# Keeping the split weights of a layer's first pass in DRAM for its second pass, in a three-layer kernel on one core

## The chip, the cores and the metric

The kernel runs on one core of a Trainium2 chip. The metric is the device time of one execution in microseconds (us), less is better. Times of single stretches come from one profiled execution.

## The reference

Linear attention for 4 batches, 8 heads, 576 tokens and 64 columns a head; then a mixture of 4 experts; then a gated feed-forward layer. With x of 2304 tokens by 512 columns after attention:

```python
# attention, per batch and head
q_s = softmax(q, axis=-1); k_s = softmax(k, axis=sequence)
x = q_s @ (k_s.T @ v)
# experts: p is 2304 x 4, w1 4 x 512 x 1024, w2 4 x 1024 x 512
p = probs / (probs.sum(-1) + 1e-9)
x = sum(p[:, e:e+1] * (relu(x @ w1[e]) @ w2[e]) for e in range(4))
# feed-forward: w_in 512 x 2048 and w_out 2048 x 512
h = x @ w_in
out = (h / (1 + exp(-1.702 * h))) @ w_out
```

w_in and w_out arrive as float64.

## The kernel before

Every product is made as if in float32: each operand is split into two float32r parts of 12 bits, hi and lo, and a product is three passes on TensorE (hi·hi, hi·lo, lo·hi). The first product of a layer runs on 2 x 2 blocks with seven block products (Winograd's form of Strassen's scheme).

**Units and passes.** A unit is 256 columns of a hidden layer: 16 units for the experts, 8 for the feed-forward layer. The tokens are taken in two passes of 1152 (two batches each); every unit is gone through once in each pass, in this order: experts pass 0 (units 0 to 15), experts pass 1 (16 to 31), feed-forward pass 0 (32 to 39), feed-forward pass 1 (40 to 47). Within a pass, a unit takes two steps, one on a pair of blocks of 256 tokens and one on a pair of 320. A step has five stages: in them stand the seven products m1 to m7 of the step (six matmuls each), and between these the second product of the step before, one tile of 128 tokens a stage (six matmuls of 512 columns each). So a unit is 84 + 54 = 138 matmuls.

**Weights of a unit.** `load_w` brings the raw float32 weights: `ra` (first product) and `rc` (second product), 512 KB each, from a pool of three buffers. From `ra` come seven parts: the blocks a11, a12, a22 and the sums s1 to s4, which `sum_w` makes on GpSimd. `hi_w1` rounds each part to its hi on ScalarE, `lo_w1` subtracts on GpSimd to give its lo. `hi_w2` and `lo_w2` do the same for the two halves of `rc`. A unit prepares the seven parts of the next one (`prepare`, in the order of the table `TWO`: a11, a12, s2 in its first step, s1, s3, a22, s4 in its second) and its own two halves of the second product in stages 1 and 3 of its first step. In pass 1 of a layer all of this is done a second time for the same weights. The very first units run ahead of the rest on one pair (`AHEAD` = 3), and their weights are prepared twice in pass 0.

**Around it.** Attention for the second pass runs as a background job in experts pass 0, the decoding of the float64 weights of the feed-forward layer as one in experts pass 1: `pump` lets the job go one turn at the end of every stage. A piece of the decode (128 x 512 values, 32 pieces) is a load `w64`, four turns of two VectorE operations each (in the last of them one on GpSimd takes the place of the second, L531), and a store. VectorE also adds up the results (`acc`, L651 and L660), makes lo of the activations (`h_lo`, L596 and L600) and the sums of block products (L574). All transfers are issued by SyncE, whose queue is taken in order.

**Order.** Up to the second unit of the feed-forward layer the program's order is kept on every engine; from there on the framework orders the instructions by priority and by its own estimate of times.

Of the kernel before, what the change touches and what calls it, by code (L numbers as in the profile page):

```python
# [8 lines left out]
F32 = mybir.dt.float32  # L9
BF16 = mybir.dt.bfloat16  # L10
F32R = mybir.dt.float32r
# [11 lines left out]
def tile_linear_attention_moe_gelu(  # L23
# [11 lines left out]
):  # L35
    """Linear attention, a mixture of experts and a gated feed-forward layer.

    A float32 operand of a product is the exact sum of two float32r parts of 12 bits, hi and lo;
    a product is hi*hi + hi*lo + lo*hi, three passes. The first product of each layer runs
    on 2 x 2 blocks with seven block products (Winograd's form of Strassen's scheme).  # L40

    Tokens of a batch are taken in the order c * 96 + p for token p * 6 + c. A pass covers two
    batches; weights come in units of 256 columns of the hidden layer.
    """
    nc = tc.nc
# [3 lines left out]
    NT, DM = out.shape  # L49
# [19 lines left out]
    accp = ctx.enter_context(tc.tile_pool(name="accp", bufs=TT))  # L69
    w1p = ctx.enter_context(tc.tile_pool(name="w1p", bufs=20))  # L70
    w2p = ctx.enter_context(tc.tile_pool(name="w2p", bufs=8))
    rawp = ctx.enter_context(tc.tile_pool(name="rawp", bufs=3))
# [38 lines left out]
    def probs_ops():  # L111
        """The normalized probabilities, each on its token's partition, as pieces by name.

        They come as [p, b, c, e]; a product with a shifted identity puts the token c * 96 + p
        into its tile of 128.
        """
        y = {}

        def pr_(_):
            n = evp.tile([SP, B, NCH, E], F32, tag="ev", name="prn")  # L120
            sh = evp.tile([SP, 3 * SP], F32, tag="ev", name="shift")
            sm = evp.tile([SP, B * NCH], F32, tag="ev", name="prs")
            y.update(sh=sh, sm=sm, f=n.rearrange("p b c e -> p (b c) e"))
            S_.dma_start(
                out=n.rearrange("p b c e -> p b (c e)"),
                in_=probs.rearrange("(b p c) e -> p b (c e)", b=B, c=NCH),
            )
            G.memset(sh, 0.0)
            G.tensor_copy(sh[:, SP : 2 * SP], ident[:SP, :SP])

        def pn(_):
            sm, f = y["sm"], y["f"]
            V.tensor_reduce(out=sm, in_=f, op=ALU.add, axis=AX.X)
            V.tensor_scalar_add(sm, sm, EPS)
            V.reciprocal(sm, sm)
            V.tensor_tensor(
                out=f, in0=f, in1=sm.unsqueeze(2).to_broadcast([SP, B * NCH, E]), op=ALU.mult
            )

        def pp(_):  # L140
            f, sh = y["f"], y["sh"]
            ps = y["ps"] = pso.tile([P, NT // P, E], F32, tag="o", name="pr_ps")
            by_tile = ps.rearrange("p (x t) e -> p x t e", t=3)
            by_group = f.rearrange("p (x g) e -> p x g e", g=4)
            for t in range(3):
                first = [(0, *divmod(t * P, SP))]
                first += [((g * SP) - t * P, g, 0) for g in range(4) if t * P < g * SP < (t + 1) * P]
                for x, (o, g, p0) in enumerate(first):
                    T.matmul(
                        by_tile[:, :, t, :], sh[:, SP + p0 - o : SP + p0 - o + P], by_group[:, :, g, :],  # L150
                        start=(x == 0), stop=(x == len(first) - 1), skip_group_check=True,
                    )

        def pc(_):
            V.tensor_copy(pr, y["ps"])

        return {"pr": pr_, "pn": pn, "pp": pp, "pc": pc}

# [1 line left out]

    KT_PATH = (0,)  # batches whose k takes its maximum on its transpose
    AHEAD = 3  # units that run on the first pair of tokens before the second is there
    LEAD = 5
# [28 lines left out]
    def attend(b, j, pool, bufs, x, small_bufs):  # L192
        """Softmax of a pair of heads and its product, x transposed into xf: its pieces by name.

        The maximum and the exponential of k are taken on k (k..) or on its transpose (K..).
        x has the tiles of k, q and v.
        """
        nm = f"{b}_{j}"
# [166 lines left out]
    def attention(todo, pool, skew):  # L365
        """Every turn a piece of each pair of heads begun; a new one every skew turns."""
        load = lambda b, j: (b, j, {x: load_attn(x, b, j, pool, 5, 2) for x in "kqv"})
# [14 lines left out]

# [1 line left out]

    X = {}

    def blocks(i, nm):
        """The seven blocks of xf[i] the products take, as pieces by name; the sums are made in place."""
        n = PAIRS[i][1]
# [31 lines left out]
    def blocks_x(g, i):  # L421
        """The blocks of the next pass, some in every stage of the steps in between."""
        ops = blocks(i, f"g{g}")
        for x in BLOCK_STAGES:
            run(ops, x)
            yield

    def to_x2(g, ti):
        """One tile of tokens of the layer's result, transposed into xf."""
        src = acc[ti]  # L430
# [10 lines left out]

# [1 line left out]

# [9 lines left out]
    insts = [*range(AHEAD), *range(NG)]  # L453
    raw, W1, W2 = {}, {}, {}

    def load_w(m, part):
        kind, e, f, *_ = units[insts[m]]
        cols = slice(f * FU, (f + 1) * FU)
# [18 lines left out]

    def sum_w(m, x):
        l, r, op = MADE[x]
        o = sump.tile([P, 2, P], F32, tag="s", name=f"{x}_{m}")  # L480
        G.tensor_tensor(out=o, in0=block_w(m, l), in1=block_w(m, r), op=op)  # L481
        sums[m, x] = o

    def hi_w1(m, x):
        W1[m, x] = tuple(w1p.tile([P, 2, P], F32R, tag="w1", name=f"{x}{r}{m}") for r in "hl")
        A.copy(W1[m, x][0], block_w(m, x))  # L486

    def lo_w1(m, x, eng):
        hi, lo = W1[m, x]
        eng.tensor_tensor(out=lo, in0=block_w(m, x), in1=hi.bitcast(F32), op=ALU.subtract)  # L490

    def hi_w2(m, c):
        W2[m, c] = tuple(w2p.tile([P, DM], F32R, tag="w2", name=f"w2{r}{m}_{c}") for r in "hl")
        A.copy(W2[m, c][0], raw[m, 1][:, c, :])  # L494

    def lo_w2(m, c, eng):
        hi, lo = W2[m, c]
        eng.tensor_tensor(out=lo, in0=raw[m, 1][:, c, :], in1=hi.bitcast(F32), op=ALU.subtract)  # L498

    def decode(src, dst, pool, nm):  # L500
        """float64 bits to the nearest float32, beyond its range clamped by the exponent."""
        n = src.shape[1]
# [28 lines left out]
        G.tensor_tensor(out=o, in0=o, in1=t.bitcast(F32), op=ALU.add)  # L531
        S_.dma_start(out=dst, in_=o)
        yield

# [1 line left out]

# [13 lines left out]
    def mm1(g, i, m, ho):  # L550
        """The first product of a layer on one block of tokens and its activation, as pieces by name."""
        n = PAIRS[i][1]
# [63 lines left out]

    # the pieces of mm1 in five stages; the last two entries run in the next step's first stage
    STAGES = {
# [5 lines left out]
    def mm2(g, ti, m, ho):  # L624
        """One tile of tokens of the second product, and its sum: as two pieces."""
        kind, e, f, pas, first, last = units[g]
# [41 lines left out]

    # what becomes of the next weights during the stages of a step, over two steps or over one
    TWO = (  # L670
# [13 lines left out]

    # the program's order is kept up to the feed-forward layer; there Tile orders it
    AUTO = 2 * NPASS * len(moe) + 2
# [18 lines left out]
    def decode_all(dec):  # L705
# [10 lines left out]
        for n, x in enumerate(todo):  # L716
            if n + 1 < len(todo):
                next(todo[n + 1])
            yield from x

    def step(k_, tiles, tail):
        """mm1 of one unit on one pair, between it the tiles of mm2 of the step before."""
        g, i, m = steps[k_]
# [34 lines left out]

    # The beginning up to the second step of the second pair, in the order of issue: piece:whose@engine;
    # _b_j is a pair of heads, a number alone a unit's weights, b a pair's blocks, s a step.  # L760
    # A bare number is so many products that keep TensorE's clock up.
    START = """
# [53 lines left out]
    def keep_warm(n):  # L816
        """TensorE's clock drops when it idles; it is kept up through the waits of the beginning."""
        for _ in range(n):
            T.matmul(hot, warm, warm, start=True, stop=True)
# [96 lines left out]
```

## Time and profile before

| | |
|---|---|
| runs | 1308.29, 1309.29, 1311.0 us; median 1309.29 |
| profiled execution | span 1308.0 us from first to last instruction; no other time is given for it |
| TensorE, VectorE, GpSimd, ScalarE busy | 95%, 78%, 55%, 45% of the span |
| moved by DMA | 98.85 MB, on average 76 GB/s |

A busy TensorE is not one at its peak, since ends of matmuls are modelled: the pace is read from the matmuls counted in a stretch, not from the busy share.

### The profile page before, as it was taken

What the parts mean: (1) busy time and instruction counts of PE and PEld (TensorE: products, weight loads), DVE (VectorE), ACT (ScalarE), POOL (GpSimd) and SP (SyncE); (2) the same over time, 40 slices, a digit from 0 to 9 for tenths busy, and PEclk for the clock granted to TensorE, in tenths of its full rate; (3) what the DMA queues carried; (4) which work ended last, traced back from release to release, by engine and by line L of the source; (5) the groups of instructions that cost most, each with busy time, mean ns of one, the idle gap of its engine ahead of it and who ended that gap; (6) DMA issues with size and microseconds to landing.
All of it is one profiled execution on the core that took longest, in us unless ns stands there. A gap on an engine that the chain in (4) does not pass through costs nothing.

```text
span 1308.0 us, 20206 instructions
## 1 busy us (share of the span) xinstructions
PE 1243.1 (95%) x7313; PEld 1097.3 (84%) x7313; DVE 1018.5 (78%) x1721; ACT 585.6 (45%) x1468; POOL 715.4 (55%) x755
## 2 busy tenths in 40 slices
PE   8788999999999998999999999999999998999998
PEld 7677888889888987888878787898799996899997
DVE  7997776666676587999999999758666669566765
ACT  4564344344433455433333333335754555654542
POOL 5686545444454475756665566547653558354430
PEclk9899999999999998999999999999999999999999
DMA  9324222222210112334433333111120112220102
GB/s 196 104 65 125 59 76 60 60 76 77 60 49 33 49 65 81 105 121 118 125 113 115 111 121 105 65 49 33 49 65 33 50 49 65 73 65 33 40 10 73
DMA packets 82899, 98.85 MB, mean 76 GB/s; under 512 B 27760, under 2 KB 59248, under 8 KB 82800
## 3 DMA queue, kind: packets, MB, share of 16 engines
q1 hardware_dynamic: 82800, 97.57, 25.8%
q8 instruction: 57, 0.93, 0.3%
q14 instruction: 42, 0.34, 0.1%
HBM read 84.45 MB, written 13.11 MB: 75 GB/s over the span
## 4 chain that ended last, share of the span: by engine, by line
PE 62%; DVE 31%; issue 3%; POOL 2%; ACT 1%; SPq 1%; DMA 0%; POOLq 0%; DVEq 0%; ACTq 0%
PE po L639 32%; PE px L544 16%; PE pz L544 8%; DVE acc L651 6%; DVE h_lo L596 6%; PE py L544 4%; DVE u L574 2%; PE p L341 1%; DVE dso L511 1%; DVE p L574 1%; DVE dso L519 1%; DVE dto L526 1%; DVE dti L526 1%; PE px L319 1%; DVE dsi L511 1%
## 5 line engine op out<-in xcount | busy, mean ns | idle before, releaser
L639 PE MATMUL po<-w2h,h_lo 128*128 128x512 f32 x864 | 340.6, 394 | 18.2 <-DVE h_lo L596 15.6
L639 PE MATMUL po<-w2h,h_hi 128*128 128x512 f32 x864 | 343.2, 397 | 5.9 <-DVE acc L651 3.5
L639 PE MATMUL po<-w2l,h_hi 128*128 128x512 f32 x864 | 343.7, 398 | 1.2 <-POOL w2l L498 1.2
L651 DVE SCALAR_TENSOR_TENSOR acc<-po,pr,acc 128x512 f32<-128x512 f32 x270 | 200.7, 744 | 85.8 <-PE po L639 85.2
L639 PEld LDWEIGHTS po<-w2h,h_lo 128*128 128x128 f32 x864 | 163.0, 189 | 63.9 <-DVE h_lo L596 23.8
L498 POOL TENSOR_TENSOR w2l<-rc,w2h 128x512 fp32r<-128x512 f32 x98 | 136.4, 1398 | 132.5 <-ACT w2h L494 132.5
L639 PEld LDWEIGHTS po<-w2h,h_hi 128*128 128x128 f32 x864 | 163.5, 189 | 28.9 <-DVE acc L651 4.1
L639 PEld LDWEIGHTS po<-w2l,h_hi 128*128 128x128 f32 x864 | 163.7, 189 | 23.6 <-POOL w2l L498 5.7
L93 ACT COPY u<-px 128x256 f32<-128x256 f32 (+1 forms) x186 | 73.9, 397 | 229.1 <-PE px L544 228.8
L574 DVE TENSOR_TENSOR u<-pz,u 128x256 f32<-128x256 f32 (+1 forms) x192 | 86.6, 451 | 57.9 <-ACT u L93 43.0
L660 DVE TENSOR_TENSOR acc<-po,acc 128x512 f32<-128x512 f32 x126 | 86.5, 687 | 49.9 <-PE po L639 49.9
L590 ACT ACTIVATE h_hi<-u 128x320 fp32r<-128x320 f32 (+1 forms) x128 | 57.0, 445 | 96.6 <-DVE u L574 96.5
L596 DVE SCALAR_TENSOR_TENSOR h_lo<-u,h_hi 128x320 fp32r<-128x320 f32 (+1 forms) x128 | 93.2, 728 | 2.8 <-ACT h_hi L590 2.7
L481 POOL TENSOR_TENSOR s<-ra 128x256 f32<-128x256 f32 x102 | 86.2, 845 | 3.7 <-DVE s1l L490 1.7
L93 ACT COPY p<-px 128x320 f32<-128x320 f32 x93 | 36.9, 397 | 100.4 <-PE px L544 100.3
L490 POOL TENSOR_TENSOR s1l<-s,s1h 128x256 fp32r<-128x256 f32 x49 | 41.2, 842 | 73.3 <-ACT s1h L486 73.3
L490 POOL TENSOR_TENSOR a11l<-ra,a11h 128x256 fp32r<-128x256 f32 x50 | 40.8, 815 | 70.1 <-ACT a11h L486 70.0
L490 POOL TENSOR_TENSOR s2l<-s,s2h 128x256 fp32r<-128x256 f32 x49 | 42.4, 866 | 56.6 <-ACT s2h L486 55.9
L494 ACT CAST w2h<-rc 128x512 fp32r<-128x512 f32 x102 | 62.6, 619 | 14.5 <-PE po L639 14.5
L596 DVE SCALAR_TENSOR_TENSOR h_lo<-p,h_hi 128x256 fp32r<-128x256 f32 (+1 forms) x64 | 48.7, 761 | 21.1 <-ACT h_hi L590 21.0
L490 POOL TENSOR_TENSOR s3l<-s,s3h 128x256 fp32r<-128x256 f32 x47 | 41.4, 881 | 43.0 <-ACT s3h L486 41.0
L408 POOL TENSOR_TENSOR xf<-xf 128x512 f32<-128x512 f32 (+1 forms) x28 | 48.3, 1724 | 21.2 <-DVE b11lg L404 10.9
(246 smaller groups left out, 3483.2 us busy)
## 6 DMA issues: line engine op xcount, KB each, us to landing
ra<-in_moe_w SPq DMA_DIRECT2D x35, 512.0 KB, 3.6
rc<-in_moe_w SPq DMA_DIRECT2D x35, 512.0 KB, 4.0
w64i<-in_moe_w_in SPq DMA_DIRECT2D x16, 512.0 KB, 5.0
w64o<-in_moe_w_out SPq DMA_DIRECT2D x16, 512.0 KB, 4.3
ra<-wi SPq DMA_DIRECT2D x16, 512.0 KB, 3.4
rc<-wo SPq DMA_DIRECT2D x16, 512.0 KB, 3.5
q<-in_q SPq DMA_DIRECT2D x16, 288.0 KB, 5.4
v<-in_v SPq DMA_DIRECT2D x32, 144.0 KB, 5.6
```

The costliest lines, as they stand in the source:

```text
L93: (eng.copy if eng is A else eng.tensor_copy)(o, i)
L481: G.tensor_tensor(out=o, in0=block_w(m, l), in1=block_w(m, r), op=op)
L490: eng.tensor_tensor(out=lo, in0=block_w(m, x), in1=hi.bitcast(F32), op=ALU.subtract)
L494: A.copy(W2[m, c][0], raw[m, 1][:, c, :])
L498: eng.tensor_tensor(out=lo, in0=raw[m, 1][:, c, :], in1=hi.bitcast(F32), op=ALU.subtract)
L544: T.matmul(ps, a[:, kk, :], b[:, kk, :], start=(start and n == 0), stop=(stop and n == 5), skip_group_check=True,)
L574: return lambda _: V.tensor_tensor(out=y[o], in0=y[ps], in1=y[o], op=ALU.add)
L590: A.activation(hi, y[c], AF.Relu)
L596: V.scalar_tensor_tensor(out=lo, in0=y[c], scalar=0.0, in1=hi.bitcast(F32), op0=ALU.max, op1=ALU.subtract)
L639: T.matmul(ps, a, b, start=(n == 0), stop=(n == 3 * FT - 1))
L651: V.scalar_tensor_tensor(out=acc[ti], in0=ps, scalar=pe, in1=acc[ti], op0=ALU.mult, op1=ALU.add)
L660: V.tensor_tensor(out=acc[ti], in0=ps, in1=acc[ti], op=ALU.add)
```

## The change

In pass 0 of a layer every split part is stored to a DRAM tensor of its own after its lo is made; in pass 1 the part is loaded from there, and no raw weights are loaded, no sums made and no parts split. hi and lo share one tile, so the pools have half as many buffers of twice the size. At most two parts wait to be stored (`put_away(2)`). The store of a decoded piece is issued two turns into the next piece instead of at its own end, and the load of the next piece one turn before that piece's first operation instead of at the beginning of the piece before. The seven parts are 256 KB each with hi and lo, the two halves 512 KB each.

```diff
-    w1p = ctx.enter_context(tc.tile_pool(name="w1p", bufs=20))
-    w2p = ctx.enter_context(tc.tile_pool(name="w2p", bufs=8))
+    w1p = ctx.enter_context(tc.tile_pool(name="w1p", bufs=10))
+    w2p = ctx.enter_context(tc.tile_pool(name="w2p", bufs=4))
...
+    of_unit = [units[g][:3] for g in insts]
+    again = [units[g][3] > 0 for g in insts]
+    kept, stores = {}, []
+
+    def new_part(m, x, pool, tag, shape):
+        t = pool.tile([P, 2, *shape], F32R, tag=tag, name=f"{x}_{m}")
+        flat = t.rearrange("p l a b -> p (l a b)").bitcast(F32)
+        u = of_unit[m]
+        if again[m]:
+            put_away(0)
+            S_.dma_start(out=flat, in_=kept[u, x])
+        elif m >= AHEAD:
+            parts[m, x] = flat
+        return t[:, 0], t[:, 1]
+
+    def store_part(m, x):
+        if m < AHEAD:
+            return
+        d = dram.tile(list(parts[m, x].shape), F32, name=f"k_{x}_{m}")
+        stores.append((d, parts.pop((m, x))))
+        kept[of_unit[m], x] = d
+        put_away(2)
+
+    def put_away(but):
+        while len(stores) > but:
+            d, flat = stores.pop(0)
+            S_.dma_start(out=d, in_=flat)
...
     def load_w(m, part):
+        if again[m]:
+            return
...
     def hi_w1(m, x):
-        W1[m, x] = tuple(w1p.tile([P, 2, P], F32R, tag="w1", name=f"{x}{r}{m}") for r in "hl")
-        A.copy(W1[m, x][0], block_w(m, x))
+        W1[m, x] = new_part(m, x, w1p, "w1", [2, P])
+        if not again[m]:
+            A.copy(W1[m, x][0], block_w(m, x))
 
     def lo_w1(m, x, eng):
+        if again[m]:
+            return
         hi, lo = W1[m, x]
         eng.tensor_tensor(out=lo, in0=block_w(m, x), in1=hi.bitcast(F32), op=ALU.subtract)
+        store_part(m, x)
...
-        S_.dma_start(out=dst, in_=o)
+        late.append(lambda: S_.dma_start(out=dst, in_=o))
         yield
...
         for n, x in enumerate(todo):
-            if n + 1 < len(todo):
-                next(todo[n + 1])
-            yield from x
+            for stage, _ in enumerate(x):
+                yield
+                if stage == 1 and late:
+                    late.pop(0)()
+                if stage == 2 and n + 1 < len(todo):
+                    next(todo[n + 1])
+        late.pop(0)()
```

`sum_w` and `lo_w2` return at once for such a unit in the same way, and `hi_w2` takes its tile from `new_part` too. Comments and descriptions are left out of the new version, which moves no instruction.

## Rows read from the trace of the kernel before

**Rows 1.** Windows by unit: busy us and instructions of PE, PEld, DVE, ACT, POOL; clock, DMA share, GB/s.
```profile
476.70:515.50 38.80, 32.02 (x176) 27.45 (x175) 34.14 (x48) 20.78 (x45) 26.21 (x23) 0.91 0.20 68
515.50:827.00 311.50, 293.16 (x1660) 252.94 (x1659) 304.37 (x478) 107.76 (x283) 195.22 (x185) 1.00 0.37 115
...
850.60:874.20 23.60, 23.60 (x140) 21.29 (x139) 13.60 (x24) 8.61 (x23) 10.55 (x14) 1.00 0.15 45
...
1075.70:1103.80 28.10, 24.90 (x140) 20.83 (x139) 27.51 (x40) 17.25 (x41) 20.90 (x18) 1.00 0.17 53
1103.80:1131.30 27.50, 25.62 (x141) 22.35 (x140) 20.10 (x35) 16.14 (x40) 17.63 (x17) 0.94 0.38 110
1131.30:1273.00 141.70, 141.70 (x829) 127.80 (x829) 93.41 (x182) 74.00 (x190) 63.55 (x72) 1.00 0.11 34
```

**Rows 2.** Groups by line and shape on VectorE, 515.5 to 827: busy us, mean ns.
```profile
L596 DVE SCALAR_TENSOR_TENSOR h_lo<-u,h_hi 128x320 fp32r<-128x320 f32 x24 | 18.1, 755 | 0.0
L596 DVE SCALAR_TENSOR_TENSOR h_lo<-p,h_hi 128x256 fp32r<-128x256 f32 x12 | 17.0, 1418 | 0.4 <-ACT h_hi L590 0.4
L512 DVE TENSOR_SCALAR dso<-dso 128x512 int32<-128x512 int32 x16 | 15.8, 986 | 0.5
L526 DVE TENSOR_TENSOR dto<-dto,dso 128x512 int32<-128x512 int32 x16 | 15.3, 954 | 0.5
L519 DVE SCALAR_TENSOR_TENSOR dso<-w64o,dso 128x512 int32<-128x512 int32 x16 | 14.0, 875 | 0.6
L596 DVE SCALAR_TENSOR_TENSOR h_lo<-u,h_hi 128x256 fp32r<-128x256 f32 x24 | 13.8, 577 | 0.0
L511 DVE TENSOR_SCALAR dso<-w64o 128x512 int32<-128x512 int32 x16 | 13.1, 821 | 0.0
...
L516 DVE TENSOR_SCALAR dso<-dso 128x512 int32<-128x512 int32 x16 | 10.4, 652 | 0.0
...
L596 DVE SCALAR_TENSOR_TENSOR h_lo<-px,h_hi 128x320 fp32r<-128x320 f32 x12 | 5.7, 479 | 0.0
...
L596 DVE SCALAR_TENSOR_TENSOR h_lo<-px,h_hi 128x256 fp32r<-128x256 f32 x12 | 4.9, 411 | 0.0
```

**Rows 3.** Instructions of the decode's tile ds, first 16 pieces: ns min/median/max, first and last start.
```profile
L511 DVE TENSOR_SCALAR dsi<-w64i x16: 419/868/1791, 483.7 to 650.5; 128x512 int32<-128x512 int32 x16
L512 DVE TENSOR_SCALAR dsi<-dsi x16: 428/844/1410, 485.5 to 651.6; 128x512 int32<-128x512 int32 x16
L516 DVE TENSOR_SCALAR dsi<-dsi x16: 408/544/1772, 489.0 to 654.4; 128x512 int32<-128x512 int32 x16
L519 DVE SCALAR_TENSOR_TENSOR dsi<-w64i,dsi x16: 691/693/1662, 490.8 to 654.9; 128x512 int32<-128x512 int32 x16
L526 DVE TENSOR_TENSOR dti<-dti,dsi x16: 691/694/1928, 494.0 to 656.9; 128x512 int32<-128x512 int32 x16
```

**Rows 4.** Groups by line on GpSimd, 515.5 to 827.
```profile
L498 POOL TENSOR_TENSOR w2l<-rc,w2h 128x512 fp32r<-128x512 f32 x24 | 36.9, 1537 | 0.0
...
L531 POOL TENSOR_TENSOR doo<-doo,dto 128x512 f32<-128x512 f32 x16 | 21.8, 1364 | 34.5 <-DVE doo L528 34.5
```

**Rows 5.** Waits, 515.5 to 827: us in total, times, longest.
```profile
PE po L639 <- DVE h_lo L596: 12.5, 15, 1.3
```

**Rows 6.** Windows of 40 us.
```profile
0.00:40.00 40.00, 33.36 (x329) 30.18 (x329) 32.05 (x68) 19.97 (x47) 22.96 (x35) 0.96 1.01 209
...
800.00:840.00 40.00, 38.99 (x228) 34.22 (x227) 35.86 (x59) 14.05 (x39) 27.09 (x27) 1.00 0.25 85
```

**Rows 7.** The DMA queue (packets, MB, share), and issues by line (KB each, median us to landing).
```profile
q1 hardware_dynamic: 82800, 97.57, 25.8%
...
rc<-in_moe_w SPq DMA_DIRECT2D x35, 512.0 KB, 4.0
...
q<-in_q SPq DMA_DIRECT2D x16, 288.0 KB, 5.4
...
wi<-doi SPq DMA_DIRECT2D x16, 256.0 KB, 3.3
```

**Rows 8.** Waits of SyncE's queue, whole span.
```profile
SPq L466 <- POOL w2l L498: 259.0, 16, 20.6
```

More of the change, by code (lines that the diff above doesn't have):

```diff
@@ L454, in tile_linear_attention_moe_gelu @@
     raw, W1, W2 = {}, {}, {}
+    of_unit = [units[g][:3] for g in insts]
[11 more added lines that the diff above has]
+        return t[:, 0], t[:, 1]
+    parts = {}
+    def store_part(m, x):
[9 more added lines that the diff above has]
+            S_.dma_start(out=d, in_=flat)
     def load_w(m, part):
+        if again[m]:
+            return
         kind, e, f, *_ = units[insts[m]]
@@ L484, in hi_w1 @@
     def hi_w1(m, x):
-        W1[m, x] = tuple(w1p.tile([P, 2, P], F32R, tag="w1", name=f"{x}{r}{m}") for r in "hl")
-        A.copy(W1[m, x][0], block_w(m, x))
+        W1[m, x] = new_part(m, x, w1p, "w1", [2, P])
+        if not again[m]:
+            A.copy(W1[m, x][0], block_w(m, x))
     def lo_w1(m, x, eng):
+        if again[m]:
+            return
         hi, lo = W1[m, x]
         eng.tensor_tensor(out=lo, in0=block_w(m, x), in1=hi.bitcast(F32), op=ALU.subtract)
+        store_part(m, x)
     def hi_w2(m, c):
-        W2[m, c] = tuple(w2p.tile([P, DM], F32R, tag="w2", name=f"w2{r}{m}_{c}") for r in "hl")
-        A.copy(W2[m, c][0], raw[m, 1][:, c, :])
+        hi, lo = new_part(m, f"w2{c}", w2p, "w2", [1, DM])
+        W2[m, c] = hi[:, 0], lo[:, 0]
+        if not again[m]:
+            A.copy(W2[m, c][0], raw[m, 1][:, c, :])
     def lo_w2(m, c, eng):
+        if again[m]:
+            return
         hi, lo = W2[m, c]
         eng.tensor_tensor(out=lo, in0=raw[m, 1][:, c, :], in1=hi.bitcast(F32), op=ALU.subtract)
+        store_part(m, f"w2{c}")
+    late = []
     def decode(src, dst, pool, nm):
```

## The prediction

> **What bounds the kernel now.** I first cut the span at the beginnings of units (the first product of each unit's first part) and read the windows by unit [rows 1]. A unit is 138 matmuls. In undisturbed stretches TensorE is busy throughout and a unit takes 23.6 us: once in experts pass 1 after the decode has ended, and the same over six units of the last pass (141.7 / 829 x 138 = 23.6) [rows 1]. That is TensorE's own pace, and no work taken from other engines goes below it. Three stretches of the second passes lie above it. Twelve units of experts pass 1 (515.5 to 827, 1660 matmuls) take 311.5 us where 12 x 23.6 = 283.2 would do: 28.3 us too long. The first unit of that pass takes 38.8 us, with TensorE idle for 38.8 - 32.0 = 6.8 of them. The first two units of the last pass take 28.1 + 27.5 = 55.6 instead of 47.2, 8.4 too long [rows 1].
>
> In the twelve units VectorE is busy 304.4 of 311.5 us, 98% [rows 1]: here the decode runs, and VectorE, not TensorE, sets the pace. TensorE's waits there are for `h_lo`, VectorE's product [rows 5]. Next I read why VectorE is so full. The same `h_lo` operation of 128x256 takes 411 ns when its first operand is in PSUM (px), and 577 and 1418 ns on average when both operands are in SBUF (u, p); 128x320 takes 479 against 755 [rows 2]. The decode's operations, all on SBUF, have averages of 652 to 986 ns [rows 2] and minima of 408 to 691 [rows 3]. Something stretches VectorE's operations on SBUF. GpSimd is busy 195.2 us in the same stretch [rows 1], and it works on SBUF too. That GpSimd's operations are what stretches them is an inference; that px is never stretched speaks for it.
>
> **The change part by part.**
>
> *Weights no longer split in the second passes.* GpSimd has 195.2 us in the twelve units, of which the 30 additions of the decode are 30 x 1.364 = 40.9 [rows 1, 4]; the remaining 154.3 us, 12.9 a unit, are sums and lo of weights (the largest group: 24 at 1537 ns [rows 4]), and they go. ScalarE loses nine copies a unit; it is busy only 107.8 of 311.5 us [rows 1], so I count nothing for it.
>
> What that gives VectorE: the stretching of `h_lo` is 24 x (755 - 479) + 12 x (1418 - 411) + 24 x (577 - 411) ns = 6.6 + 12.1 + 4.0 = 22.7 us [rows 2]. In the decode, five of the seven operations of a piece average 821 + 986 + 652 + 875 + 954 = 4288 ns [rows 2] against minima of 419 + 428 + 408 + 691 + 691 = 2637 [rows 3], 1.65 us a piece, 49.5 for 30 pieces (the first pieces taken to be as the last 16). Together 72 us. Shared out by GpSimd's busy time, the weights cause 154.3 / 195.2 = 79%, 57 us. VectorE then needs 304.4 - 57 = 247 us, 87% of the 283.2 of TensorE's pace, and TensorE is the bound again.
>
> Not all of the 28.3 us comes back, since VectorE's queue is in order and decode operations stand ahead of `h_lo`. The row nearest to 87% is the window 800 to 840: VectorE at 35.86 / 40 = 90%, 228 matmuls where the full pace gives 40 / 23.6 x 138 = 234, a loss of 2.5% [rows 6]. At 13.60 / 23.6 = 58% no time is lost [rows 1]. On the line between them 87% loses 2.3%, 6.4 us of 283.2. I take 28.3 - 6.4 = 22 us gained; bounds 28 (no loss) and, if the stretching is caused by the decode's own additions in larger part, the case "late decode" below.
>
> The Trainium skill ("SBUF — State Buffer", Who interferes with whom) says that a VectorE instruction with two SBUF inputs and a GpSimd instruction that reads SBUF exclude each other for a whole instruction; by it the 30 additions that stay could each hold VectorE for their full 1.364 us, so that it needs an estimated 304.4 - 72 + 41 = 273 us, 96%, and on the same line the loss is 8.4 us and the sum 2 us worse. The rows here (411 ns with PSUM, up to 1418 with SBUF) agree with its kind of conflict. I keep the share by busy time, because an addition comes at the end of a piece and the next piece's operations are a turn away.
>
> *Beginnings of passes.* Units 16, 40 and 41 have 6.8 + 8.4 = 15.2 us of idle or lost time [rows 1]. There GpSimd makes the sums of the new pass's blocks between weights (26.2 of 38.8 us busy, 20.9 of 28.1), and the granted clock is at 0.91 and 0.94 of full on average [rows 1]. Bounds 0 and 15.2; since most of the waiting chain (block sums, their splits, new accumulators) stays, I take a third: 5 us. The other six units of the last pass are at TensorE's pace and gain nothing.
>
> *Loads of split parts.* A second-pass unit now loads 7 x 256 + 2 x 512 KB = 2.88 MB instead of 1.05. Nearest rows for landing: 3.3 us for 256 KB, 4.0 us for 512 KB [rows 7]. The cover is the ring of buffers. With ten tiles and seven parts a unit, s1 of the next unit takes the tile of this unit's a11, which is free after the first product of the second step, and is first used in stage 1 of the next step: five or six stages, at 2.36 us a stage over 12 us. a11, a12 and s2 have more. The halves of the second product have four tiles, two a unit: theirs are free a whole step earlier. SyncE waits for nothing but these releases, so it runs ahead of the program by two stages or more. I count nothing. Without that cover (issue only at its place in the program, stage 3) the second half of w2 has two stages, 4.7 us, against 4.0 us to land.
>
> In volume: 97.57 MB take 25.8% of the 16 engines now [rows 7], 289 GB/s at full use. In the twelve units 115 GB/s at a share of 0.37 [rows 1] become about 115 + 1.83 MB / 23.6 us = 193 GB/s, a share of 0.62.
>
> *Stores in the first passes.* Nine a unit, on SyncE; each waits for GpSimd's lo of that part, and behind it stand raw loads and attention's. SyncE already waits 259 us for `w2l` before loads of `rc` without harm [rows 8]. A store is issued two parts after its own, and a tile comes round after ten, so neither blocks. The hand-written beginning has stores in front of raw loads of units that are used soon after: I put 1 us there, bounds 0 and 3.
>
> *Decode's store and load later.* The store leaves SyncE free sooner, which helps. The load of a piece moves from four turns ahead to one turn (2.36 us) in the program, against 4.0 us to land [rows 7]; the lead of SyncE hides it: ahead of it in the queue stand only releases that come 2.5 stages (6 us) before its use. Counted as nothing; if not hidden, the case "late decode".
>
> Sum against the span: 1308.0 - 22 - 5 + 1 = 1282. The median of the runs is 1.3 us above the span, so 1283 us.
>
> **The rivals.**
>
> *Late decode.* Each load of a piece is late by 4.0 - 2.36 = 1.6 us and VectorE waits: 30 x 1.6 = 49 us, so it is occupied 247 + 49 = 296 us, more than 283.2. Then only 311.5 - 296 = 15, less the in-order loss of 6, some 9 us come back there, and the time is 1308 - 9 - 5 + 1 + 1.3 = 1296. For it: the move itself. Against: the lead of SyncE.
>
> *Late weights, slower than before.* In the second passes TensorE waits for loads at every unit. The gain of 26 us is used up at 26 / 24 = 1.1 us a unit. If the nine loads went one after the other, they would need 7 x 3.3 + 2 x 4.0 = 31.1 us a unit [rows 7], 7.5 above the pace: 1283 + 24 x 7.5 = 1463. Against it: in the first 40 us 209 GB/s were moved [rows 6], while one load of 288 KB in 5.4 us is 55 GB/s [rows 7], so about four are under way at a time. Milder, and likelier: a landing of 8 us instead of 4 under the heavier traffic, with SyncE not ahead, makes w2 late by 8 - 4.7 = 3.3 us: 1283 + 24 x 3.3 = 1362. The Trainium skill ("DMA: Bandwidth & Descriptors", Anatomy of one DMA) gives about 2.0 us fixed and the bytes at 436 GB/s for a transfer issued by GpSimd; one after another that is an estimated 24.6 us a unit, 1 us above the pace, and about 1307 in all. The rows of the first 40 us show that transfers overlap here, so I give that little.
>
> *Late raw loads in the first passes.* Stores ahead in SyncE's queue delay `ra` and `rc`; at 1 us for each of the 21 other unit preparations the time is 1283 + 21 = 1304. Against it: the 259 us of harmless waiting [rows 8].
>
> *No change.* VectorE's operations are stretched by something other than GpSimd (the decode's access pattern, say), it stays full, and the beginnings stay: 1309. Against it: the same operation on pieces of one form takes from 691 to 1928 ns (L526) and from 419 to 1791 (L511) [rows 3].
>
> **How the numbers follow.** Chances: forecast 0.68, late decode 0.12, late weights 0.11, late raw loads 0.05, no change 0.04. The forecast's own range goes from everything recovered, 1308 - 28 - 15 + 1.3 = 1266, to 1308 - 11 + 1 + 1.3 = 1299 (half of the 22, nothing at the beginnings). With late decode and up to 1300 that holds 0.80; what is left out is slower or nearly unchanged. A change within 0.2% (2.6 us) is about what a measurement of this kernel cannot tell from none. Faster: forecast, late decode and most of late raw loads, 0.83; same 0.05; slower 0.12.
>
> **What would show it.** Right: units of experts pass 1 at 23.6 to 24.2 us; `h_lo` from p near 411 ns; the decode's operations near their minima; VectorE at 85 to 92% there; GpSimd nearly idle but for the additions; no wait of TensorE for a DMA. Wrong: waits of `po` or `px` for a transfer, VectorE idle before L511 for `w64`, or first-pass units longer than now, as they would also be if the framework's own order in the feed-forward layer turned out worse.

## The result and the profile after

The changed kernel takes 1277.08 us (median of 4 runs, 1274.89 to 1279.81) against 1310.14 before (4 runs): a ratio of 0.9743, 95% interval 0.9724 to 0.9763. The span of the profiled execution fell from 1308.0 to 1277.9 us, by 30.1; the profiled execution of the changed kernel is the slowest of its four (1279.81 us).

Cut at the beginnings of units (the first product of each), the 30.1 us lie here, after minus before: unit 3 begins 1.3 us later; units 3 to 15 +0.3 in all; unit 16 -2.3; units 17 to 28 -27.9; units 31 and 32 +1.2 and +1.8; units 39 and 40 -1.5 and -3.0; every other unit within 0.1. Windows by unit of the changed kernel, columns as in [rows 1]:

```profile
478.30:514.80 36.50, 31.98 (x177) 27.19 (x175) 31.08 (x48) 17.41 (x35) 11.35 (x7) 0.91 0.32 103
514.80:798.30 283.50, 283.50 (x1658) 255.57 (x1657) 253.87 (x478) 70.17 (x175) 38.75 (x30) 1.00 0.62 202
...
845.60:870.30 24.70, 23.80 (x139) 21.15 (x139) 16.40 (x28) 9.85 (x25) 10.55 (x11) 1.00 0.35 118
...
1049.90:1076.60 26.70, 24.71 (x141) 21.03 (x140) 26.07 (x41) 14.36 (x33) 13.13 (x8) 1.00 0.38 120
1076.60:1101.00 24.40, 23.84 (x139) 21.16 (x139) 15.58 (x34) 12.68 (x30) 0.00 (x0) 1.00 0.69 205
1101.00:1242.70 141.70, 141.70 (x830) 127.78 (x829) 85.54 (x182) 56.27 (x138) 0.00 (x0) 1.00 0.38 119
```

The second row is the answer to 515.5 to 827 in [rows 1]: the same twelve units in 283.5 us instead of 311.5. TensorE has no idle time in it, VectorE's busy time fell from 304.4 to 253.9 us, GpSimd's from 195.2 to 38.8, and the DMA engines' share rose from 0.37 to 0.62. Units 41 to 46 (the last row) take 141.7 us as before.

Groups by line on VectorE in that stretch (busy us, mean ns of one), against [rows 2]:

```profile
L645 DVE SCALAR_TENSOR_TENSOR h_lo<-u,h_hi 128x320 fp32r<-128x320 f32 x24 | 17.8, 742 | 0.0
L645 DVE SCALAR_TENSOR_TENSOR h_lo<-u,h_hi 128x256 fp32r<-128x256 f32 x24 | 16.2, 675 | 0.0
...
L575 DVE TENSOR_TENSOR dto<-dto,dso 128x512 int32<-128x512 int32 x16 | 11.1, 693 | 0.5
L568 DVE SCALAR_TENSOR_TENSOR dso<-w64o,dso 128x512 int32<-128x512 int32 x16 | 11.1, 692 | 0.5
...
L645 DVE SCALAR_TENSOR_TENSOR h_lo<-p,h_hi 128x320 fp32r<-128x320 f32 x12 | 10.8, 902 | 2.7 <-ACT h_hi L639 2.7
...
L561 DVE TENSOR_SCALAR dso<-dso 128x512 int32<-128x512 int32 x16 | 6.8, 428 | 0.6
...
L565 DVE TENSOR_SCALAR dso<-dso 128x512 int32<-128x512 int32 x16 | 6.7, 417 | 0.0
L560 DVE TENSOR_SCALAR dso<-w64o 128x512 int32<-128x512 int32 x16 | 6.6, 415 | 0.0
...
L645 DVE SCALAR_TENSOR_TENSOR h_lo<-p,h_hi 128x256 fp32r<-128x256 f32 x12 | 5.0, 419 | 0.9 <-ACT h_hi L639 0.9
```

The reader sees the decode's operations at the minima of [rows 3] (986 to 428 ns, 954 to 693, 821 to 415), and `h_lo` from p at 419 instead of 1418. `h_lo` from u is still stretched (742 and 675), and `h_lo` from p of 320 columns is stretched only now (902), where it took 485 before:

```profile
L596 DVE SCALAR_TENSOR_TENSOR h_lo<-p,h_hi 128x320 fp32r<-128x320 f32 x12 | 5.8, 485 | 0.0
```

The additions of the decode stay on GpSimd, and they now meet `h_lo`: 18 `h_lo` run beside one, six of each of these three forms, and together they take 17.4 us more than unstretched ones (415 and 484 ns) would. No other `h_lo` is stretched.

All waits of TensorE for a transfer after the first pass of the experts (us in total, times, longest), and what SyncE issued just before (begin, us, issue):

```profile
PE po L688 <- DMA w<-k_w: 0.9, 1, 0.9
```
```profile
851.18 0.32 SPq L488 DMA_DIRECT2D k_a<-a  x1
851.55 0.42 SPq L469 DMA_DIRECT2D w<-k_w  x1
853.88 0.32 SPq L488 DMA_DIRECT2D k_a<-a  x1
855.80 0.32 SPq L488 DMA_DIRECT2D k_s<-s  x1
856.17 0.42 SPq L469 DMA_DIRECT2D w<-k_w  x1
```

There is one, in unit 31, which begins at 845.6: the load of w2's second half was issued at 856.17, right behind stores of two parts of the next layer (853.88 and 855.80), and TensorE waited for it until 861.0.

### The profile page after: what moved, and what is told of

The parts are those of the page before. It is cut to its first block, busy times and chain, and to the rows that moved or that the text cites. A ratio compares the mean times of both kernels' runs of the same rounds, so it can differ in the third digit from the quotient of the medians.

```text
span 1277.9 us, 20369 instructions
## 1 busy us (share of the span) xinstructions
PE 1234.6 (97%) x7313; PEld 1101.5 (86%) x7313; DVE 945.0 (74%) x1721; ACT 512.1 (40%) x1252; POOL 418.1 (33%) x443
## 4 chain that ended last, share of the span: by engine, by line
PE 86%; DVE 10%; DMA 1%; issue 1%; SPq 1%; POOL 1%; ACT 1%; ACTq 0%; DVEq 0%
PE po L688 44%; PE px L593 22%; PE pz L593 11%; PE py L593 5%; DVE h_lo L645 1%; PE p L344 1%; PE px L322 1%; DVE acc L700 1%; DMA q<-in_q 1%; DVE dg L260 1%; DVE t3lg L407 1%; SPq L189 1%; DVE xf L411 0%; DVE t2lg L407 0%; DVE u L623 0%
## 5 line engine op out<-in xcount | busy, mean ns | idle before, releaser
L688 PE MATMUL po<-w,h_hi 128*128 128x512 f32 x1728 | 546.0, 397 | 6.5 <-DVE acc L700 3.6
L688 PEld LDWEIGHTS po<-w,h_hi 128*128 128x128 f32 x1728 | 303.3, 190 | 48.2 <-DVE acc L700 4.2
L688 PE MATMUL po<-w,h_lo 128*128 128x512 f32 x864 | 338.8, 392 | 5.5 <-DVE h_lo L645 3.1
L688 PEld LDWEIGHTS po<-w,h_lo 128*128 128x128 f32 x864 | 163.3, 189 | 45.5 <-DVE h_lo L645 4.8
L531 POOL TENSOR_TENSOR s<-s,s 128x256 fp32r<-128x256 f32 x98 | 77.8, 797 | 106.5 <-ACT s L525 101.3
L544 POOL TENSOR_TENSOR w<-rc,w 128x512 fp32r<-128x512 f32 x50 | 66.5, 1335 | 72.7 <-ACT w L538 72.6
L580 POOL TENSOR_TENSOR doo<-doo,dto 128x512 f32<-128x512 f32 x16 | 20.7, 1292 | 131.6 <-DVE doo L577 122.4
L593 PE MATMUL px<-t4hg,a 128*128 128x256 f32 (+1 forms) x256 | 61.8, 297 | 2.0 <-ACT u L96 1.9
L593 PE MATMUL pz<-t1hg,s 128*128 128x256 f32 (+1 forms) x256 | 62.9, 301 | 0.0
L593 PE MATMUL px<-t2hg,s 128*128 128x256 f32 (+1 forms) x256 | 62.4, 299 | 0.0
L593 PE MATMUL pz<-b22hg,s 128*128 128x256 f32 (+1 forms) x256 | 61.8, 297 | 0.5 <-DVE u L623 0.4
```

Of the source, the lines that this page charges most:

```text
L593: T.matmul(ps, a[:, kk, :], b[:, kk, :], start=(start and n == 0), stop=(stop and n == 5), skip_group_check=True,)
L688: T.matmul(ps, a, b, start=(n == 0), stop=(n == 3 * FT - 1))
```

## The experiments

All medians are of kernels timed in turn with the kernel before on the same chip; ratios are to that kernel (its medians were 1310.1 to 1311.1 us). "The twelve units" are units 17 to 28, 311.5 us before and 283.5 after.

### Does GpSimd's reading stretch VectorE?

The changed kernel, with idle work on GpSimd wherever a second pass no longer prepares a part:

```
+    def idle_work(big):
+        n = 4 if big else 2
+        pool, tag = (rawp, "raw") if big else (sump, "s")
+        o = pool.tile([P, n, P], F32, tag=tag, name="idle")
+        G.tensor_tensor(out=o, in0=kvbd[:, :n], in1=kvbd[:, 4 - n :], op=ALU.subtract)
...
     def sum_w(m, x):
         if again[m]:
-            return
+            return idle_work(False)
```

(the same in `lo_w1`, and with True in `lo_w2`). Expected:

> The changed kernel, but wherever a second-pass part is no longer summed or split, GpSimd does a subtraction of the same size on idle tiles (128x256 or 128x512, inputs and output in SBUF) that nobody reads. Theory (VectorE was stretched by GpSimd's operations that read SBUF): units of the second experts pass go back from 23.6 to 25 to 26 us, VectorE to 97% or more of that stretch, the whole to 1300 to 1309 us. Rival (the gain came from the copies taken from ScalarE, or from weights that no longer wait for a chain of three engines): units stay at 23.6 us and the whole within 3 us of 1277.

Measured: 1359.84 us, ratio 1.0384 (1.0362 to 1.0405), far above either forecast. By units the theory's number was there: 304.4 us for the twelve units. The rest was an accident of the experiment: in the feed-forward layer, where the framework orders the instructions, the idle work had no inputs to wait for and 82 subtractions were put in front of GpSimd's sums for the next pass (ScalarE waited 59.4 us for one of these), and unit 39 alone took 86.9 us.

Filling instead of subtracting, three fills `G.memset(o, 1.0)` for a subtraction:

> As the run with idle subtractions, but GpSimd fills the idle tiles with a constant instead, three fills for each subtraction, so that it is busy about as long without reading SBUF. If reading is what stretches VectorE: units of the second experts pass at 23.6 us, the whole within 3 us of 1277. Rival (any busy GpSimd, its writes too): units at 25 to 26 us, the whole at 1300 or more.

Measured: 1287.82 us, 0.9831 (0.9803 to 0.9859); the twelve units 283.5 us, and again unit 39 too long, 41.2 us. So both were run again with idle work in the experts' second pass only (`return units[insts[m]][0] == "moe" and idle_work(False)`).

> The idle subtractions on GpSimd as before, but in the second pass of the experts alone, where the program's order is kept (in the feed-forward layer they had been moved together in front of GpSimd's needed work). Theory (reads of SBUF by GpSimd stretch VectorE): 304 us again for the twelve units of the decode against 283.5, the whole 21 us above the changed kernel, 1295 to 1300. Rival (the earlier 304 us hung on something else in that run): 283.5 and 1277.

Measured: 1297.79 us, 0.9896 (0.9881 to 0.9910). The window of the twelve units, and three groups of VectorE in it:

```profile
513.40:817.20 303.80, 290.21 (x1659) 253.71 (x1658) 298.20 (x478) 71.02 (x175) 181.49 (x183) 1.00 0.58 188
```
```profile
L573 DVE SCALAR_TENSOR_TENSOR dso<-w64o,dso 128x512 int32<-128x512 int32 x16 | 17.0, 1060 | 0.6
L566 DVE TENSOR_SCALAR dso<-dso 128x512 int32<-128x512 int32 x16 | 13.5, 847 | 0.5
...
L650 DVE SCALAR_TENSOR_TENSOR h_lo<-p,h_hi 128x256 fp32r<-128x256 f32 x12 | 9.2, 763 | 0.0
```

No load, no copy and no wait was put back, only subtractions that nobody reads, and 20.3 of the 28.0 us are back, with VectorE busy 298.2 of 303.8 us (98%). TensorE waits for no transfer in this stretch, only for `h_lo` and the sums of block products. The total is 20.7 us above the changed kernel.

> The idle fills on GpSimd, in the second pass of the experts alone. If only reads stretch VectorE: 283.5 us for the twelve units and the whole within 3 us of 1277. Rival (writes too): above 290 us and 1284.

Measured: 1274.88 us, 0.9724 (0.9710 to 0.9739). Window and groups:

```profile
511.10:794.60 283.50, 283.50 (x1659) 255.61 (x1658) 262.00 (x478) 70.46 (x175) 211.69 (x495) 1.00 0.62 203
```
```profile
L575 DVE SCALAR_TENSOR_TENSOR dso<-w64o,dso 128x512 int32<-128x512 int32 x16 | 11.1, 692 | 0.6
...
L568 DVE TENSOR_SCALAR dso<-dso 128x512 int32<-128x512 int32 x16 | 8.8, 549 | 0.5
L567 DVE TENSOR_SCALAR dso<-w64o 128x512 int32<-128x512 int32 x16 | 8.2, 515 | 0.0
```

GpSimd is busier here (211.7 us) than in the run with subtractions (181.5), and TensorE loses nothing. The operation with two inputs in SBUF stays at 692 ns, where subtractions made it 1060; those with one input go only from 415 and 428 to 515 and 549. The Trainium skill ("SBUF — State Buffer", Who interferes with whom) says that a VectorE instruction with two SBUF inputs contends with a GpSimd instruction that reads SBUF and not with one that only writes it. The trace agrees: 1060 ns beside subtractions, 692 beside fills. The same section of the Trainium skill says that VectorE in its two-port modes, which `tensor_scalar` can enter, contends with GpSimd. The 515 and 549 ns would fit that; in which mode these operations ran no run shows.

### What the later store of decoded pieces is worth

The kernel before with the decode's later store and load alone:

```
-        S_.dma_start(out=dst, in_=o)
+        late.append(lambda: S_.dma_start(out=dst, in_=o))
```

(and the loop of `decode_all` as in the change).

> The kernel before with the later store and later load of the decode alone. Theory (the decode's transfers bind nothing while VectorE is full): within 3 us of the kernel before. Rival (the later store frees the queue of SyncE and brings part of the gain): at least 5 us faster. The case of the late decode: slower by up to the 9 to 13 us that late pieces cost.

Measured: 1312.05 us, 1.0014 (1.0002 to 1.0026); the twelve units 311.9. Alone it brings nothing. Now the changed kernel with both at their old places:

> The changed kernel with the store and load of decoded pieces where they were before. Theory (SyncE's lead over the program is what hides the loads, and it stays about two stages when it waits for each piece's addition): within 3 us of 1277. Rival (the store at the end of a piece holds the loads of split parts back): TensorE waits for transfers in the second experts pass, and the whole is 5 us or more above 1277.

Measured: 1288.53 us, 0.9833 (0.9809 to 0.9858), 11.4 above the changed kernel: the rival. Window of the twelve units, and waits in it:

```profile
512.70:808.90 296.20, 286.00 (x1660) 254.87 (x1659) 254.54 (x478) 70.27 (x175) 38.75 (x30) 1.00 0.58 194
```
```profile
PE po L688 <- DMA w<-k_w: 10.2, 10, 1.9
...
SPq L581 <- POOL doo L580: 116.3, 16, 9.6
SPq L581 <- POOL doi L580: 100.4, 14, 9.5
SPq L469 <- PE px L593: 4.1, 7, 1.9
```

The same waits of SyncE in the changed kernel:

```profile
SPq L469 <- PE px L593: 89.1, 31, 6.8
SPq L581 <- POOL doo L580: 63.3, 13, 6.9
SPq L581 <- POOL doi L580: 50.9, 11, 6.2
```

In the changed kernel SyncE waits 114 us for additions of the decode and 89 us for tiles to come free (L469): 31 times it stands at a load before the tile is free, so that it issues the load at the earliest moment. With the store at its old place it waits 217 us for additions and hardly ever for a tile (4.1 us): when it comes to a load, the tile is free already. VectorE does the same work in both (254 us). TensorE then waits ten times for w2. Which of the two moves counts was asked with the store late and the load where it was before:

```
         for n, x in enumerate(todo):
+            if n + 1 < len(todo):
+                next(todo[n + 1])
             for stage, _ in enumerate(x):
...
-                if stage == 2 and n + 1 < len(todo):
-                    next(todo[n + 1])
```

> The changed kernel with the later store of decoded pieces, but their load where it was before, at the beginning of the piece before. Theory (it is the store at its old place, waiting for GpSimd's addition of the current piece, that takes SyncE's lead away and makes loads of w2 late): units of the second experts pass at 23.6 us, the whole within 3 us of 1277. Rival (the early load of a piece delays the parts behind it): units at 24 to 25 us as with both at their old places, the whole at 1282 to 1289.

Measured: 1277.16 us, 0.9747 (0.9725 to 0.9769); the twelve units 283.8. The store does it; the place of the load is worth 0.3 us there at most.

### The wait in unit 31

```
         if again[m]:
-            put_away(0)
+            if x == "s4":
+                put_away(0)
             S_.dma_start(out=flat, in_=kept[u, x])
```

> The changed kernel, but a load of a kept part no longer first sends off all stores that wait; that is done once a unit, at s4. Theory (in unit 31 the load of the second half of w2 stood behind stores of the next layer's first parts, and TensorE waited 0.9 us for it): unit 31 goes from 24.8 us to 23.6 to 23.9, nothing else changes, the whole within 3 us of 1277 (the difference of about 1 us can't be told from the whole). Rival (the landing itself was slow): unit 31 stays at 24.8.

Measured: 1275.62 us, 0.9735 (0.9718 to 0.9753). The window of unit 31:

```profile
844.70:868.30 23.60, 23.60 (x140) 21.28 (x139) 16.45 (x29) 9.76 (x25) 10.59 (x11) 1.00 0.30 102
```

23.6 us against 24.7 (24.8 by its own beginnings). The load of w2's second half was issued 10.6 us after the beginning of the unit, behind the stores that loads sent ahead of themselves; here it is issued after 6.0 us, and the wait is gone. The stores made the load late, but whether TensorE then waits hangs on its landing too. Six other profiles here have the load after 10.6 us as well, and unit 31 took from 23.6 us (both runs with idle work in the experts alone) to 24.2 (the two runs with the decode's load at its old place).

### The feed-forward layer's share

Parts kept in the experts alone (`again[m]`, `parts` and `store_part` ask for `units[...][0] == "moe"` too).

> The changed kernel with parts kept for the experts alone; the feed-forward layer prepares its weights in both passes. Theory (the feed-forward layer's gain is 4.5 us in units 39 and 40, the rest of its second pass is at TensorE's pace; without stores of its first parts unit 31 loses its 1.2 us): units 39 and 40 at 28.1 and 27.5 us again, unit 31 at 23.6, the whole 2 to 5 us above 1277. Rival (the stores cost the feed-forward layer more than they bring): at or below 1275.

Measured: 1280.84 us, 0.9763 (0.9747 to 0.9779). Units 39 and 40:

```profile
1046.90:1078.00 31.10, 26.18 (x140) 22.03 (x139) 30.47 (x43) 17.28 (x41) 23.14 (x18) 0.95 0.15 50
1078.00:1103.50 25.50, 24.22 (x141) 21.15 (x140) 17.73 (x32) 15.51 (x39) 15.68 (x17) 1.00 0.40 117
```

Together 56.6 us, against 55.6 before [rows 1] and 51.1 after. Unit 31 is at 23.6. So keeping the feed-forward layer's parts is worth 5.5 us at the beginning of its last pass (GpSimd 23.1 and 15.7 us busy there against 13.1 and 0). It was forecast as 28.1 and 27.5 us; the sum came, the two sizes didn't (31.1 and 25.5, the first at a mean granted clock of 0.95). The whole is 3.8 us longer, inside the forecast, but the intervals of the two ratios overlap (0.9747 to 0.9779 and 0.9724 to 0.9763).

### Beyond the change: the first three units

As the run with one sending off a unit, and the units that run ahead store their parts too, so that their second preparation is a load:

```
-    again = [units[g][3] > 0 for g in insts]
+    again = [units[g][3] > 0 or AHEAD <= m < 2 * AHEAD for m, g in enumerate(insts)]
...
-        elif m >= AHEAD:
+        else:
             parts[m, x] = flat
...
-        if m < AHEAD:
-            return
```

(and a load whose own store still waits sends it off first).

> As the run that sends off stores once a unit, and in addition the parts of the first three units, which run ahead on the first pair, are stored and loaded for the second pair instead of being prepared a second time. TensorE is idle some 8 us between 60 and 141 us, where VectorE and GpSimd are up to 90% busy. Theory (they bind there too): unit 3 begins 3 to 8 us earlier than its 140 us, the whole at 1269 to 1274. Rival (SyncE's queue, in which loads of parts now wait for tiles and for stores, holds back what the beginning needs): unit 3 at 141 us or later, the whole at 1277 or more.

Measured: 1272.21 us, 0.9707 (0.9688 to 0.9727): the fastest kernel here. Its four runs (1269.69 to 1273.59 us) lie below the five of the run it builds on (1275.05 to 1276.38). Two windows of its beginning, and the longest wait in it:

```profile
80.00:100.00 20.00, 19.92 (x120) 17.63 (x119) 16.54 (x28) 11.11 (x25) 9.53 (x6) 1.00 0.83 269
100.00:136.00 36.00, 32.72 (x180) 29.16 (x179) 19.11 (x34) 13.07 (x28) 10.83 (x14) 1.00 0.69 208
```
```profile
PE po L687 <- DMA w<-k_w: 2.7, 1, 2.7
```

From 80 to 100 us GpSimd is busy 9.5 us where it was 17.0 in the run it builds on, and TensorE 19.9 where it was 17.3. Unit 3 begins at 135.7 us instead of 141.7 (in the other profiles, the kernel before among them, at 139.5 to 141.8). One load of a kept half of w2 is late there, by 2.7 us; why was not tried.

## Why the prediction was right

**The place of the gain.** 1283 us were forecast, 1277.1 measured. The gain was forecast where it came: 22 us in the twelve units (28.0 measured), 5 at the beginnings of passes (units 16, 39 and 40: 2.3 + 1.5 + 3.0 = 6.8). The two units that the prediction calls 40 and 41, the first two of the last pass, are 39, the last of the pass before, and 40. A later beginning of unit 3 and longer units 31 and 32 took some 4.6 us of it back, where 1 was set aside: outside the twelve units 4 us were forecast and 2.2 came. The step from [rows 2, 3] to "GpSimd's operations stretch VectorE's" was an inference there; the idle subtractions show it for 20.3 of the 28.0 us. No run was made for the other 7.7. Most of them are VectorE's busy time as well, which is 6.2 us shorter than before (298.2 against 304.4) for the same 478 instructions. Idle subtractions wait for nothing, so GpSimd is a little less busy than before (181 against 195 us) and meets other operations (`h_lo` from p at 763 ns, not 1418), and ScalarE's copies stayed out. It stays open how these share it.

**VectorE's load.** 247 us forecast, 253.9 measured; 87% and 90% of the time. That this came near is in part luck. The prediction shared the stretching out by GpSimd's busy time and let 79% of it go both in the decode (39 of 49.5 us) and in `h_lo` (18 of 22.7). By the sums of the groups the decode's operations lost 50.5 us (162.0 to 111.5), all that was counted, and `h_lo` only 4.7 (65.3 to 60.6), as the additions that stay now stretch it by 17.4 us. What counted was which operations an addition meets, not its share of the busy time, and the two errors nearly cancel. (VectorE's operations overlap a little, so its busy time fell by 50.5 us and not by the 55.2 of the groups.)

**The mis-sized term: the loss at 87%.** The prediction kept 6.4 of the 28.3 us back, on a line through the window 800 to 840 [rows 6]. At 90% nothing was lost: TensorE 283.5 of 283.5 us. That window was a mixture: the decode ended at 827, so it held 27 us with VectorE full (99%), which lost 1.0 us of TensorE, and 13 with it busy 70%, which lost nothing:

```profile
800.00:827.00 27.00, 25.99 (x149) 22.50 (x148) 26.73 (x44) 9.51 (x27) 16.39 (x16) 1.00 0.28 95
827.00:840.00 13.00, 13.00 (x82) 11.72 (x81) 9.13 (x16) 4.54 (x12) 10.69 (x12) 1.00 0.18 63
```

Its average of 90% was the load of neither part. With fills VectorE was busy 92% (262.0 of 283.5 us), and still nothing was lost.

**The step that failed: "Decode's store and load later ... counted as nothing".** The prediction saw that the later store frees SyncE, and priced only the load. The store was the part that mattered: without it 12.7 of the 28.0 us are lost (296.2 us against 283.5), through the mechanism of the rival "late weights", a load of w2 held up in SyncE's queue. The sentence that SyncE "waits for nothing but these releases" doesn't hold, even in the changed kernel: there it waits 114 us at the stores of pieces, but stays far enough ahead of the loads. By itself the edit is worth nothing (1.0014): in the kernel before TensorE waits for no transfer in the twelve units, only for VectorE and once, for 0.8 us, for GpSimd.

**Late decode.** The rival didn't come. Loads of pieces took 5.1 and 5.6 us to land in the median, not 4.0, and still VectorE waits for none of them in the twelve units.

**Late weights in the changed kernel.** They occur once, 0.9 us in unit 31, behind stores of parts that wait for GpSimd. A landing of 512 KB took 5.5 us in the median in the twelve units (202 GB/s moved), not 4.0 as in [rows 7]; the lead of SyncE covered it.

**Stores in the first passes.** 1 us was set aside for the beginning. Units 4 to 15 differ by at most 0.03 us from before, although 175 GB/s are moved there, and unit 3 begins at 139.5 us in one run with stores and at 140.8 in the run without any (the late decode alone): nothing in these runs charges the later beginning to the stores, and a cost of about 1 us isn't excluded (nine profiles with these stores: 139.5 to 141.8; the kernel before: 139.5). The Trainium skill ("SBUF — State Buffer", Who interferes with whom) says that DMA never contends with a compute engine; the unchanged units (0.03 us) agree.

**Beginnings.** Their size varies with the clock. Unit 16 took 36.5 us in the changed kernel, 35.2 with the store late only and 32.8 with fills, at mean granted clocks of 0.91, 0.95 and 1.00:

```profile
478.00:513.20 35.20, 30.68 (x176) 26.04 (x175) 30.99 (x48) 17.30 (x35) 11.29 (x7) 0.95 0.31 98
```
```profile
478.30:511.10 32.80, 29.54 (x177) 24.74 (x175) 31.53 (x48) 17.26 (x35) 26.87 (x51) 1.00 0.31 106
```

The records show one of TensorE's two levels at a time: 1.2 GHz for 6.8 us of the first, 3.4 us of the second and never in the third; TensorE was idle for 36.5 - 32.0 = 4.5 us in the first, 4.5 in the second and 3.3 in the third. In the 10 us before the fall TensorE was busy for 7.8 us in the first and 7.0 in the second; in the third it was busy for 7.6 us from 490.6 to 500.6, and the clock stayed up. Unit 32's extra 1.8 us go with 6.8 us at the low level instead of 3.4. Why one run falls and another doesn't was not tried. So part of what came at the beginnings is chance.

## What to carry to other kernels

When VectorE is full, look at the spread of one operation on one shape: if the form with an operand in PSUM is quick and the form with both in SBUF is stretched, VectorE may be paying for GpSimd's reads of SBUF, as here, and moving GpSimd's work into DMA can free VectorE (304.4 to 253.9 us). Idle work on GpSimd, once with reads and once with writes alone, tests it. A load that replaces computing is only as early as the queue that issues it: list what the instructions ahead of it wait for, and move a store that waits for an engine behind the loads. Read a loss at some load of an engine from a stretch of one regime, not from an average over two.

## What was not expected of the hardware

Nine loads a unit, 2.88 MB every 23.6 us, beside the decode's traffic left TensorE at its full pace at a DMA share of 0.62, with 256 KB landing in 3.2 to 4.6 us and 512 KB in 5.5. Three times as many fills as subtractions, with GpSimd busy for 212 of 283.5 us, cost TensorE nothing, where subtractions with GpSimd busy for 181 us cost 20.3.
